# A recurrent attention and a mixture of experts in one kernel: tokens laid out eight to a partition, one stream of transposes, one state per head, and a running maximum

## The chip, the core and the metric

One NeuronCore of a Trainium2 chip. The metric is the device time of one execution in microseconds (us), lower is better. TensorE (PE) multiplies, PEld is its weight load, VectorE is DVE, ScalarE is ACT, GpSimd is POOL; SP issues DMAs. Each engine runs its own instructions in order.

## The reference

```python
r, k, v: (4, 8, 768, 48) float32     # batch, heads, tokens, head dim; w, u: (8, 48), w in 0.85 to 0.95
for t in range(S):
    cur = einsum('bhd,bhe->bhde', u[None] * kt, vt)
    y[:, :, t] = einsum('bhd,bhde->bhe', rt, state + cur)
    state = w[None, :, :, None] * state + einsum('bhd,bhe->bhde', kt, vt)
x = y.transpose(0, 2, 1, 3).reshape(3072, 384)
logits = x @ phi                                   # phi (384, 32): 8 experts x 4 slots
d = exp(logits - logits.max(0)); d /= d.sum(0)     # over the tokens, for each slot
slot_input = (d.T @ x).reshape(8, 4, 384)
slot_out[e] = maximum(slot_input[e] @ w1[e], 0) @ w2[e]   # w1 (384, 1024), w2 (1024, 384)
c = exp(logits - logits.max(1)); c /= c.sum(1)     # over the slots, for each token
out = c @ slot_out                                 # (3072, 384)
```

A softmax does not change when the same number is taken from all its logits, so a kernel may take away any maximum, or none where the logits are small. The first part is a linear recurrence: with k scaled by a falling power of w and r by the opposite one, a chunk of 128 tokens is a masked 128x128 product (A, then A times v) plus r times the state of the chunks before it.

## The kernel before

Work goes by head pairs: m counts 4 batches x 4 pairs, 16 in all; each pair's 768 tokens are split in two halves of 384 (L = 3 chunks of 128), i counting 32 half-units. The 768 tokens of a head lie six to a partition (J = 6); v lies three to a partition in each half.

- **Tables** (`table`, L175, L177): W[0] and W[1] hold the powers of w, from logarithms by Exp. `scale` (L212) multiplies k and r by them and casts to bf16, on GpSimd but for the first pair.
- **Transposes**: `t_pe` (L219) turns k and r into kT and rT, `t_evac` (L225, ScalarE) puts the tokens in order while copying; `b_pe` (L231) and `b_evac` (L236, VectorE) turn kT back into kn, now in order. `prod_f` (L241) multiplies k and r elementwise for the diagonal term.
- **v** is cast by ScalarE (`v_cast`, L250) and put in order on TensorE by products with shifted permutation matrices Q3 (`v_pe`, L265, nine per half), copied out by L271.
- **Recurrence**: `a_pe` (L280) and the mask (`mask_f`, L285); `m_pe` (L306) sums k times v into states Mb of 128x96, two heads side by side, of which `z_evac` (L320, L324) masks the two diagonal blocks with bmask; the state of the first half is carried into the second one by Z0, decayed by wT. `dv` (L326) is v times the diagonal term. `y_pe` (L336, L347, L349) sums y in Yb, `y_evac` (L356) copies it into x.
- **Routing** (`route`), eight half-units later: transposes of x (L371, L380), logits with phi (L364), Exp without a maximum (L386), its transpose into LexpT (L393, L397), and the dispatch (L404) with the sum acc (L412), once per half batch.
- **After the loop**: the last two half batches of routing, the normalised slot inputs uns (L517, L519), the experts (L535 and w1, L541 and L543, transposes L552, L553, then L557 and w2), row sums (L545), and the output: 24 products (L581) alternately scaled by VectorE (L583) and ScalarE (L585), and seven DMAs.

The order on each engine is the program's order, written out by hand: a loop over i interleaves the stages of half-units i, i+1 and i+2. All loads of k, r and v come from SP's queue, batch by batch into three buffers; the weights (cast to bf16 by the DMA) from GpSimd's queue, counted out by W_AT behind given half-units, w2 into buffers that k, r and v no longer need. PSUM is eight banks: T0, T1, Ab (two), Mb, Yb, Xb, Vb. A tile of two banks is one tile to the dependences between engines.

Of the kernel before, what the change touches and what calls it, by code (L numbers as in the profile page):

```python
# [9 lines left out]
def kernel(  # L10
# [24 lines left out]
    G = 2  # L35
    L = nC // G
    T = L * C
    P2 = 2 * D
    nN = Nn // C
    nG = B * G  # L40
    nU = B * nQ
    nH = nU * G
    J = S // C
    JV = T // C

# [4 lines left out]
    ALU = mybir.AluOpType  # L50

# [7 lines left out]
    wk = ctx.enter_context(tc.tile_pool(name="wk", bufs=3))  # L59
    psb = ctx.enter_context(tc.tile_pool(name="psb", bufs=1, space=bass.MemoryType.PSUM))  # L60


    RW = H * J * D
    NR = 3
    EG = E // 2
    raw = [big.tile([128, 3 * RW], f32, name=f"raw{j}") for j in range(NR)]
    eW2 = nF * Dm
    w1_all = big.tile([128, E, nM, F], bf, name="w1_all")

    def w2_of(e):  # L70
        g, j = divmod(e, EG)
        return raw[1 + g][:].bitcast(bf)[:, j * eW2:(j + 1) * eW2].rearrange("p (y d) -> p y d", y=nF)

    def raw_of(which, b):
        return raw[b % NR][:, which * RW:(which + 1) * RW]

    T0 = psb.tile([128, 1024], bf, name="T0")
    T1 = psb.tile([128, 1024], bf, name="T1")
    Ab = psb.tile([128, 2, 512], f32, name="Ab")
    Mb = psb.tile([128, 512], f32, name="Mb")  # L80
    Yb = psb.tile([128, 512], f32, name="Yb")
    Xb = psb.tile([128, 512], f32, name="Xb")
    Vb = psb.tile([128, 512], f32, name="Vb")
    Xh = Xb[:].bitcast(bf)
    xT_p = Xh[:, 0:Dm]
    lg_p = Xb[:, 192:192 + L * ES].rearrange("p (c s) -> p c s", c=L)
    le_p = Xh[:, 640:640 + T]
    ds_p = Mb[:, 384:384 + (nM + 1) * ES]


    LexpT = cst.tile([128, Nn], bf, name="LexpT")
    early = LexpT[:, 0:2 * (2 * H * D + 128)].bitcast(f32)
    w_row = early[0:1, 0:H * D]
    lnw = early[:, H * D:2 * H * D]
    one_f = early[0:1, 2 * H * D:2 * H * D + 128]
    warm = LexpT[:, 2048:2560]
    wu = cst.tile([8, 128], f32, name="wu")
    wu3 = wu[:].rearrange("q (e s) -> q e s", s=64)
    phi_f = cst.tile([128, nM, ES], f32, name="phi_f")
    O(act.preload_act_table_set("natural_log_exp_and_others"))  # L100
    O(sp.dma_start(out=w_row, in_=w.rearrange("(o h) d -> o (h d)", o=1)))
    O(dve.memset(one_f, 1.0))
    O(dve.memset(warm, 0.0))
    O(dve.memset(wu[:], 1.0))
    O(act.dma_start(out=wu3[0:4, :, 0:D], in_=w.rearrange("(q e) d -> q e d", e=2)))
    O(act.dma_start(out=wu3[4:8, :, 0:D], in_=u.rearrange("(q e) d -> q e d", e=2)))

    def load_kr(which, src, b, h0, h1):
        O(sp.dma_start(out=raw_of(which, b).rearrange("p (h x) -> p h x", h=H)[:, h0:h1, :],
                       in_=src[b, h0:h1].rearrange("h (p j) d -> p h (j d)", j=J)))  # L110

    def load_v(b, h0, h1):
        O(sp.dma_start(out=raw_of(2, b).rearrange("p (h x) -> p h x", h=H * G)[:, h0 * G:h1 * G, :],
                       in_=v[b, h0:h1].rearrange("h (g p j) d -> p (h g) (j d)", g=G, j=JV)))

    def load_batch(b, step):
        for h0 in range(0, H, step):
            load_kr(0, k, b, h0, h0 + step)
            load_kr(1, r, b, h0, h0 + step)
            load_v(b, h0, h0 + step)  # L120

    load_batch(0, 2)
    load_batch(1, 2)
    O(sp.dma_start(out=phi_f[:], in_=moe_phi.rearrange("(mo p) s -> p mo s", p=128)))
    load_batch(2, H)

    def load_w(n, y0=0, y1=nF):
        if n < E:
            O(pool.dma_start(out=w1_all[:, n, :, :],
                             in_=moe_w1[n].rearrange("(p mo) f -> p mo f", p=128)))  # L130
        else:
            O(pool.dma_start(out=w2_of(n - E)[:, y0:y1, :],
                             in_=moe_w2[n - E].rearrange("(p y) d -> p y d", p=128)[:, y0:y1, :]))

    def keep_warm(n, cols=512):
        for _ in range(n):
            O(pe.matmul(Yb[:, 0:cols], warm[:, 0:128], warm[:, 0:cols], start=True, stop=True))


    s_i = cst.tile([128, J], i32, name="s_i")  # L140
    O(pool.iota(s_i, pattern=[[-1, J]], base=T - 1, channel_multiplier=-J))
    ident_f = cst.tile([128, 128], f32, name="ident_f")
    O(pool.memset(ident_f[:], 0.0))
    O(pool.affine_select(out=ident_f[:], in_=ident_f[:], compare_op=ALU.not_equal, fill=1.0, base=0,
                         pattern=[[-1, 128]], channel_multiplier=1))
    QW = 2 * C + JV - 1 + C
    Q3 = cst.tile([128, QW], bf, name="Q3")
    O(pool.memset(Q3[:], 0.0))
    O(pool.affine_select(out=Q3[:], in_=Q3[:], compare_op=ALU.not_equal, fill=1.0, base=JV - 1,
                         pattern=[[-1, QW]], channel_multiplier=JV))  # L150
    mask_ut = cst.tile([128, 128], f32, name="mask_ut")
    O(pool.memset(mask_ut[:], 0.0))
    O(pool.affine_select(out=mask_ut[:], in_=mask_ut[:], compare_op=ALU.is_ge, fill=1.0, base=0,
                         pattern=[[-1, 128]], channel_multiplier=1))

    sk = cst.tile([128, J], f32, name="sk")
    O(dve.tensor_copy(sk[:], s_i[:]))
    O(dve.tensor_scalar(out=sk[64:128, :], in0=sk[64:128, :], scalar1=float(T), scalar2=None, op0=ALU.add))
    sr = cst.tile([128, J], f32, name="sr")
    O(dve.tensor_scalar(out=sr[:], in0=sk[:], scalar1=-1.0, scalar2=-1.0, op0=ALU.mult, op1=ALU.add))  # L160
    NKR = 3
    kr_t = [cst.tile([128, 2, J, 128], bf, name=f"kr{j}") for j in range(NKR)]
    for t in kr_t:
        O(dve.memset(t[:].rearrange("p a j (e s) -> p (a j e) s", s=64)[:, :, D:64], 0.0))
# [3 lines left out]
    keep_warm(5)  # L168
    O(pe.matmul(Xb[:, 0:H * D], one_f, w_row, start=True, stop=True))
    O(act.activation(out=lnw, in_=Xb[:, 0:H * D], func=AF.Ln))  # L170
    W = [cst.tile([128, nQ, J, P2], f32, name=f"W{j}") for j in range(2)]

    def table(j, q):
        e = (sk, sr)[j]
        O(dve.tensor_mul(W[j][:, q], lnw[:, None, q * P2:(q + 1) * P2].to_broadcast([128, J, P2]),  # L175
                         e[:, :, None].to_broadcast([128, J, P2])))
        O(act.activation(out=W[j][:, q], in_=W[j][:, q], func=AF.Exp))  # L177

    table(0, 0)
    table(1, 0)  # L180
    bmask = cst.tile([128, P2], f32, name="bmask")
    ones = cst.tile([128, 128], bf, name="ones")
    ucol = cst.tile([128, nQ, 2], bf, name="ucol")
    Le_t = [cst.tile([128, L, 128], bf, name=f"Le{j}") for j in range(2)]
    uns = cst.tile([128, nM, 2, EG, 32], bf, name="uns")
    O(pool.memset(bmask[:], 0.0))
    O(pool.memset(bmask[0:64, 0:D], 1.0))
    O(pool.memset(bmask[64:128, D:P2], 1.0))
    O(pool.memset(ones[:], 1.0))
    O(pool.memset(ucol[:], 0.0))  # L190
    for t in Le_t:
        O(pool.memset(t[:], 0.0))
    O(pool.memset(uns[:], 0.0))
    O(pe.transpose(Mb[:, 0:8], wu[:], ident_f[0:8, 0:8]))
# [423 lines left out]
```

## Time and profile before

| | |
|---|---|
| timed runs | 148.05, 148.68, 150.45 us, median 148.68 us |
| profiled execution | span 146.5 us from the first to the last instruction; the page states no other time for it |
| TensorE / weight loads | 105.9 us (72%) / 81.6 us, 1719 products |
| VectorE | 101.9 us (70%), 200 instructions |
| ScalarE | 83.8 us (57%), 176 |
| GpSimd | 56.5 us (39%), 68 |
| DMA | 31.77 MB moved, HBM read 39.38 MB, written 4.72 MB |
| mean granted TensorE clock | 0.947 |

Busy time is a share of the whole span and so an average over stages: a preparation to 15 us, the loop to 111 us, the last routing to 117 us, the experts to 130 us, the output to the end. Products are pipelined on TensorE, and the duration of one says little of what a further one costs; the distance between starts does. A wait is put down to the instruction that came last.

### The profile page before, as it was taken

To read this page: it belongs to the slowest core of one execution; us is meant where nothing else is said; L and a number is where in the kernel's file an instruction comes from. 1 tells how busy PE (TensorE), PEld (TensorE's weight loads), DVE (VectorE), ACT (ScalarE), POOL (GpSimd) and SP (SyncE) were. 2 spreads that over 40 slices of the span, in tenths; PEclk is the share of its full clock that TensorE was granted. 3 is DMA by queue.
4 is the path that set the end of the run, shared out by engine and by line. 5 is a ranking of instruction groups with operands and counts; after the bars stand their busy time and mean duration, and the time that the engine had idled before them with its cause. 6 is when DMAs were issued, how large, how long until landed. Compare 5 with 4: busy or idle time off the path is not lost. (4 is left out here: it accounts for less than half of the span.)

```text
span 146.5 us, 4187 instructions
## 1 busy us (share of the span) xinstructions
PE 105.9 (72%) x1719; PEld 81.6 (56%) x1719; DVE 101.9 (70%) x200; ACT 83.8 (57%) x176; POOL 56.5 (39%) x68
## 2 busy tenths in 40 slices
PE   6495795748478995987788689689596579956500
PEld 1144664546367784875777577569475437534300
DVE  5355779869999999599589689689883414228710
ACT  3327565757547886687588498398475411027610
POOL 7433333359995874576449279000000000000000
PEclk9999559999999999999999999999999959999975
DMA  4999999999940199999999999999999500006994
GB/s 96 337 372 375 370 364 376 382 327 386 368 145 2 20 190 215 214 183 214 175 174 158 184 200 172 216 215 214 215 216 206 104 0 4 0 0 269 415 416 190
DMA packets 20764, 31.77 MB, mean 217 GB/s; under 512 B 1289, under 2 KB 17674, under 8 KB 20746
## 3 DMA queue, kind: packets, MB, share of 16 engines
q0 software_dynamic: 2448, 12.58, 44.1%
q1 hardware_dynamic: 18274, 18.93, 37.4%
q8 instruction: 13, 0.21, 0.6%
q14 instruction: 5, 0.04, 0.1%
q10 hardware_dynamic: 24, 0.00, 0.0%
HBM read 39.38 MB, written 4.72 MB: 301 GB/s over the span
## 5 line engine op out<-in xcount | busy, mean ns | idle before, releaser
L212 POOL TENSOR_TENSOR kr<-raw,W 128x576 bf16<-128x576 f32 x30 | 41.9, 1412 | 31.1 <-PE T L219 15.2
L285 DVE TENSOR_TENSOR AT<-Ab,mask_ut 128x768 bf16<-128x768 f32 x32 | 30.4, 951 | 3.3 <-PE Ab L280 3.3
L265 PE MATMUL Vb<-v_bf,Q 128*128 128x96 bf16 x288 | 18.1, 210 | 7.3 <-ACT v_bf L250 7.3
L265 PEld LDWEIGHTS <-Q 128*128 128x128 bf16 x288 | 16.2, 100 | 11.5 <-issue 11.0
L225 ACT COPY kT<-T 128x768 bf16<-128x768 bf16 x16 | 12.7, 796 | 14.3 <-PE T L219 14.0
L219 PE MATMUL T<-ident,kr 128*128 128x128 bf16 x192 | 16.8, 228 | 4.3 <-POOL kr L212 4.3
L356 ACT CAST x<-Yb 128x288 bf16<-128x288 f32 x32 | 13.1, 409 | 4.6 <-PE Yb L349 4.6
L219 PEld LDWEIGHTS <-kr 128*128 128x128 bf16 x192 | 12.5, 103 | 5.1 <-POOL kr L212 4.6
L271 ACT CAST vn<-Vb 128x288 bf16<-128x288 f32 x32 | 13.1, 410 | 3.7 <-PE Vb L265 2.1
L241 DVE TENSOR_TENSOR prod<-T,kT 128x768 bf16<-128x768 bf16 x16 | 15.2, 948 | 0.1
L225 ACT COPY rT<-T 128x768 bf16<-128x768 bf16 x16 | 12.7, 797 | 3.4 <-PE T L219 2.9
L326 DVE TENSOR_TENSOR dv<-vn,Mb 128x288 bf16<-128x288 bf16 x32 | 14.2, 444 | 0.0
L236 DVE COPY kn<-T 128x768 bf16<-128x768 bf16 x16 | 8.9, 554 | 7.2 <-PE T L231 4.1
L280 PE MATMUL Ab<-rT,kT 64*128 64x128 bf16 x192 | 11.1, 222 | 2.2 <-DVE AT L285 2.1
L324 DVE TENSOR_TENSOR Z<-Mb,bmask 128x192 bf16<-128x192 f32 x32 | 11.1, 348 | 0.7 <-PE Mb L310 0.7
L306 PE MATMUL Mb<-vn,kn 128*128 128x96 bf16 (+2 forms) x80 | 11.6, 245 | 0.0
L250 ACT CAST v_bf<-raw 128x576 bf16<-128x576 f32 x16 | 10.8, 675 | 0.0
L336 PE MATMUL Yb<-vn,AT 128*128 128x48 bf16 x192 | 10.4, 186 | 0.1
L349 PE MATMUL Yb<-dv,ident 128*128 128x288 bf16 x32 | 9.2, 289 | 0.6
L347 PE MATMUL Yb<-Z,rT 128*128 128x96 bf16 x80 | 8.9, 205 | 0.5 <-DVE Z L324 0.5
L336 PEld LDWEIGHTS <-AT 128*128 128x128 bf16 x192 | 7.0, 97 | 3.6 <-DVE AT L285 0.2
L380 ACT COPY xT<-Xb 128x384 bf16<-128x384 bf16 x18 | 8.8, 486 | 0.3 <-PE Xb L371 0.2
(120 smaller groups left out, 198.9 us busy)
## 6 DMA issues: line engine op xcount, KB each, us to landing
w_all<-in_moe_w_dram POOLq DMA_DIRECT2D x8, 768.0 KB, 8.4
raw<-in_moe_w_dram POOLq DMA_DIRECT2D x7, 768.0 KB, 14.5
raw<-in_k_dram SPq DMA_DIRECT2D x8, 288.0 KB, 5.1
raw<-in_r_dram SPq DMA_DIRECT2D x8, 288.0 KB, 5.5
raw<-in_v_dram SPq DMA_DIRECT2D x8, 288.0 KB, 5.6
raw<-in_k_dram SPq DMA_DIRECT2D x2, 1152.0 KB, 8.9
raw<-in_r_dram SPq DMA_DIRECT2D x2, 1152.0 KB, 10.7
raw<-in_v_dram SPq DMA_DIRECT2D x2, 1152.0 KB, 9.9
```

Of the source, the lines that this page charges most:

```text
L212: O(eng.tensor_mul(kr[:, j].rearrange("p j (h s) -> p j h s", s=64)[:, :, :, 0:D], src, W[j][:, q].rearrange("p j (h d) -> p j h d", h=2)))
L219: O(pe.transpose(bank[:, x * C:(x + 1) * C], kr[:, j, x, :], ident[:]))
L225: O(act.copy(t[:].rearrange("p (s j) -> p s j", j=J), bank[:, 0:S].rearrange("p (j s) -> p s j", j=J)))
L241: O(dve.tensor_mul(pr[:].rearrange("p (s j) -> p s j", j=J), T1[:, 0:S].rearrange("p (j s) -> p s j", j=J), st["kT", m][:].rearrange("p (s ...
L265: O(pe.matmul(Vb[:, c * P2:(c + 1) * P2], Q3[:, o:o + C], vb[:, :, g, j, :], start=(j == 0), stop=(j == JV - 1)))
L271: O(act.copy(vn[:].rearrange("p c e d -> p (c e d)"), Vb[:, 0:L * P2]))
L280: O(pe.matmul(Ab[:, e, c * C:(c + 1) * C], kT[s, t], rT[s, t]))
L285: O(dve.tensor_mul(AT[:], Ab[:, :, 0:T].rearrange("p e (c t) -> p e c t", c=L), mask_ut[:, None, None, :].to_broadcast([128, 2, L, C])))
L306: O(pe.matmul(o, kn[:, g * L + c, :], vc, start=first, stop=True, skip_group_check=True))
L326: O(dve.tensor_mul(dv[:], st["v", i][:].rearrange("p c e d -> p (c e) d"), Mb[:, 288:288 + 2 * L, None].to_broadcast([128, L * 2, D])))
L336: O(pe.matmul(Yb[:, o:o + D], AT[:, e, c, :], vn[:, c, e, :], start=first, stop=False, skip_group_check=True))
L356: O(act.copy(st["x", n][:, :, q * P2:(q + 1) * P2], Yb[:, 0:L * P2].rearrange("p (c e) -> p c e", c=L)))
```

## The change

The first part is rewritten; the experts and the output keep their form.

- Each batch is three **tiles** x of eight tokens per partition for two heads at once (heads q and q+4 side by side: e is 0 or 1). A tile holds eight chunks of 128 tokens; a head pair's six chunks run over the tiles' borders. Seven tiles fit in the buffer; 12 tiles x 3 DMAs of 384 KB.
- A **stream of 60 steps**, five per tile: k, r and v are transposed (24 products), k and v transposed back (16). A step is eight transposes into one of two banks T and a copy out of it. The copies move two bf16 as one 4-byte element. `more` drains the stream at four places of a unit; GpSimd scales k and r, and now also casts v, one tile ahead.
- A **unit** is a head pair with all 768 tokens; the powers of w are centred on token 384, so no decay between halves is needed (Z0, wT and bmask go).
- **Compact states**: each head has its own 64x48 block on its own 64 partitions, five sums of chunks per pair (KV, RZ), made by 64-column products and used by 64-row ones; one ScalarE copy instead of masks on VectorE.
- **Running maximum**: per batch the largest logit (VectorE reduction, transpose, reduction, broadcast by a product), taken away in the Exp; the sum acc of the batches before is rescaled by fac. Routing runs once per batch.
- LexpT is laid out so that later weight loads read neighbouring elements; experts, transposes and output use separate PSUM tiles in place of the two banks of Ab.
- Matmuls in the program: 1915, against 1719; VectorE rows 142 against 198, ScalarE 131 against 181.

```diff
-    G = 2; L = nC // G; T = L * C; J = S // C      # six tokens per partition, two halves
+    J = 8; R = C // J; nX = nQ * nC // J; L = nC // 2
...
+    def step(n):
+        t, kind = divmod(n, 5)
+        bank = n % 2
+        Tb = T[bank]
+        if kind < 3:
+            kr = kr_t[kind][t % NK]
+            for j in range(J):
+                O(pe.transpose(Tb[:, j * C:(j + 1) * C], kr[:, j].rearrange("p e s -> p (e s)"), ident[:]))
+            o = wk.tile([128, J * C], bf, name=("kT", "rT", "vT")[kind], bufs=(3, 3, 1)[kind])
+            st[kind, t] = o
+            O(act.copy(o[:].bitcast(f32).rearrange("p (g j c) -> p g j c", g=J, j=J),
+                       Tf[bank].rearrange("p (j g c) -> p g j c", g=J, j=J)))
+            if kind == 1:
+                ...                                 # pr: VectorE, r (PSUM) times kT, 128x1024
+            return
+        src = st[0 if kind == 3 else 2, t]
+        for g in range(J):
+            O(pe.transpose(Tb[:, g * C:(g + 1) * C], src[:, g * C:(g + 1) * C], ident[:]))
+        ...                                         # kind 3: kn by VectorE; kind 4: vn by ScalarE
+    KV = {0: (0, 3), 1: (0, 2), 2: (0, 1), 3: (3, 2), 4: (3, 1)}
+    RZ = {1: (2,), 2: (1,), 3: (0,), 4: (0, 4), 5: (0, 3)}
+    def m_pe(i):
+        for c, (s0, n) in KV.items():
+            for e in range(2):
+                s = slice(64 * e, 64 * e + 64)
+                o, vc = Mb[s, s0 * D:(s0 + n) * D], vn[:, kap, e, 0:D]
+                ...
+                O(pe.matmul(o, kn[:, sl.start + 64 * e:sl.start + 64 * e + 64], vc, ...))
+        ...                                         # diagonal term: six 2-column products
+    def z_evac(i):
+        O(act.copy(Z[:], Mb[:, 0:nZ * D]))
+        O(dve.tensor_mul(dv[:], ...))               # 128x576
+    def y_pe(i):
+        ...                                         # 12 products AT x v into Yb[:, e]
+        for c in range(1, nC):
+            for z in RZ[c]:
+                for e in range(2):
+                    O(pe.matmul(Yb[:, e, c * D:(c + 1) * D], st[1, t][s, sl], Z[s, z * D:(z + 1) * D], ...))
+        ...                                         # two products with dv
+    def max_a(b):
+        O(dve.tensor_reduce(out=mx[:], in_=lg_p, axis=AX.X, op=ALU.max))
+        O(pe.transpose(Xb[0:1, 0:128], mx[:], ident_f[:]))
+    def max_b(b):
+        O(dve.tensor_reduce(out=g_row[:, 0:1], in_=Xb[0:1, 0:128], axis=AX.X, op=ALU.max))
+        if b:
+            O(dve.tensor_max(g_row[:, 0:1], g_row[:, 0:1], g_row[:, 1:2]))
+        O(pe.matmul(Xb[:, 128:129], one_f[:], g_row[:, 0:1], start=True, stop=True))
+    # max_c: nG = -maximum; le_ev: Exp with bias nG, fac; disp_ev: acc = acc * fac + D_p
+    W_AT = {5: 2, 6: 1, 7: 1, 8: 2, 9: 1, 10: 1, 11: 2}      # weight DMAs behind the scaling of tile t
+    def target(i, part):
+        if i < 0:
+            return 4 * (i + LEAD) + part + 1        # LEAD = 3: twelve steps ahead of unit 0
+        return 4 * LEAD + (15 * (4 * i + part + 1)) // 16
+    for i in range(-LEAD, nU):
+        b, q = divmod(i, nQ)
+        a_pe(i + 1, 0); mask_f(i + 1, 0)
+        more(target(i, 0))
+        y_pe(i); y_evac(i)
+        more(target(i, 1))
+        if b >= 1 and q == 0: lg_pe(b - 1)
+        m_pe(i + 1); z_evac(i + 1)
+        a_pe(i + 1, 1); mask_f(i + 1, 1)
+        if b >= 1 and q == 0: max_a(b - 1)
+        more(target(i, 2))
+        if b >= 1 and q == 0: max_b(b - 1)
+        if b >= 1 and q == 1: le_t(b - 1); let_ev(b - 1); disp(b - 1); disp_ev(b - 1)
+        if i >= 0 and q >= 1: xt_pe(b, q - 1); xt_ev(b, q - 1)   # 12 transposes of 64 columns
+        more(target(i, 3))
+        if b >= 1 and q == 0: max_c(b - 1); le_ev(b - 1)
...
-    hb = [[Ab[:, 0, :], Ab[:, 1, :]], [Vb[:], Yb[:]]]
+    hb = [[Yb[:, 0, :], Tf[1]], [Mb[:], Tf[0]]]
...
-    ob = [T1[:].bitcast(f32), Ab[:, 0, :], Ab[:, 1, :], T0[:].bitcast(f32), Yb[:], Xb[:]]
+    ob = [Tf[0], Tf[1], Yb[:, 0, :], Xb[:], Ab[:, 0, :], Mb[:]]
```

## The prediction

> **What bounds the kernel now.** I read the page first (its slices and its groups), then busy time by stage, then the timeline of one stretch of the main loop and of the end.
>
> ```profile
> PE   6495795748478995987788689689596579956500
> DVE  5355779869999999599589689689883414228710
> PEclk9999559999999999999999999999999959999975
> DMA  4999999999940199999999999999999500006994
> ```
>
> Forty slices of 3.66 us. The DMA engines are full to slice 11 (k, r, v), rest, are full again to 112 us (weights), and once more at the end (output). VectorE is the fullest engine from slice 9 to slice 29. The granted TensorE clock is halved in slices 5 and 6.
>
> ```profile
> core 0: us, PE busy (x) PEld busy (x) DVE busy (x) ACT busy (x) POOL busy (x), PEclk, DMA share, GB/s
> 15.00:44.00 29.00, 19.96 (x325) 16.46 (x322) 25.21 (x44) 17.52 (x33) 18.80 (x14) 0.88 1.02 338
> 44.00:111.00 67.00, 55.52 (x1092) 46.68 (x1089) 56.25 (x111) 48.85 (x109) 30.90 (x33) 1.00 0.91 177
> 117.00:130.00 13.00, 11.53 (x152) 7.06 (x148) 3.33 (x6) 1.19 (x2) 0.00 (x0) 0.87 0.01 1
> ```
>
> The loop stage (15 to 111 us) is what the change rewrites. VectorE is 84 to 87% busy there. The waits list has 15.2 us of POOL L212 behind PE L219: GpSimd is mostly ahead. The starts of L285 give the pace: the ninth stands at 43.56 us, the last at 108.72, so 24 half-units cost some 2.8 us each, 5.6 us per head pair.
>
> ```profile
> L285 DVE TENSOR_TENSOR AT<-Ab,mask_ut 128x768 bf16<-128x768 f32 x32 | 30.4, 951 | 3.3 <-PE Ab L280 3.3
> L326 DVE TENSOR_TENSOR dv<-vn,Mb 128x288 bf16<-128x288 bf16 x32 | 14.2, 444 | 0.0
> ```
>
> ```profile
> 62.15 0.34 PE L280 MATMUL Ab<-rT,kT 64*128 64x128 bf16 x6
> 62.42 0.32 PE L336 MATMUL Yb<-vn,AT 128*128 128x48 bf16 x6
> 62.59 0.24 PE L347 MATMUL Yb<-Z,rT 128*128 128x96 bf16 x2
> 70.11 0.41 PE L404 MATMUL Mb<-Le,x 128*128 128x32 bf16 x9 [1.17 <-DVE dv L326]
> 124.85 4.77 PE L557 MATMUL Mb<-raw,W 128*32 128x384 bf16 x64 [0.34 <-DVE W L553]
> ```
>
> The two VectorE rows give a line: 288 elements 444 ns, 768 elements 951 ns, so 140 ns and 1.056 ns per element. The starts of the TensorE groups give prices that durations hide: six L280 in 0.27 us (45 ns each, two 64-row halves into two banks), six L336 in 0.17 us (28 ns). In the same way a 128x128 transpose costs 57 ns, a 32-column L404 29 ns, a 2-column L310 25 ns, a 288-column L349 120 ns. L404 shows a stall: TensorE runs in order, and at a boundary of the routing it waits for VectorE.
>
> **The head.** VectorE prepares two tables of 768 instead of 576 elements (0.95 for 0.75 us) and a few small operations, so the first scaling starts at about 8.8 instead of 7.57 us. Two scalings (0.95 each), six small ones (L196: 0.17 us), a table (0.95) and its exponential (ScalarE's line through L356, 288 elements 409 ns, and L225, 768 elements 797 ns, gives 0.8) put GpSimd's first scaling at 13.6. Before unit 0 has its turn TensorE must transpose k and r of tile 2, so GpSimd first does four scalings of 768 elements (L212: 1.41 us for 576, so 1.85), one cast of v and the fills of Le and uns (L193: 0.75 us for 768, so 1.7 with ones). The cast is not in the trace: at least a fill (0.75), at most a scaling (1.88); I take 1.3, a single input. 13.6+7.4+1.3+1.7 = 24.0, with the transposes **24.5 us**. After that GpSimd owes 5.0 us per tile and 0.6 us per weight issue (L129), 0.94 tiles per unit: not the pace.
>
> **A unit of the new loop** (one head pair, all 768 tokens; 16 of them). Removed: 18 permuting matmuls and 12 + 6 transposes, the Z masks (L324 2 x 0.35, L320 0.32), v_bf and half of the small copies. Added: 3.75 steps of eight transposes, 0.46 us each; Y has 12 AT products (0.34), 14 state products of 64 rows by 48 columns, two of 288 columns (0.24); M has ten 64-column products and six of 2 columns (0.15); X has 12 half-width transposes (three units of four). These 36 partial-array instructions are not in the trace in this form. From below: windows of 1 us show 30 of L557 (32-column weights, neighbours in different column groups) between 125 and 126 us, 33 ns for 384 columns. From above: L557's mean, 4.77/64 = 75 ns. I take 25 to 30 ns, since neighbours alternate halves and stream at most 144 columns: Y 0.93, M 0.45, X 0.36.
>
> TensorE's sequence in an ordinary unit: A 0.27, step 0.46, Y 0.93, step 0.46, M 0.45, A 0.27, step 0.46, X 0.36, step 0.46 = 4.12 us. VectorE's work is 2 x 0.95 (masks), 0.75 (dv, 576 elements), and per tile 1.22 (pr, 1024) and 0.69 (kn; L553: 0.69 for the same bytes): 4.1 us per unit against 5.3 before. The tighter ring runs through both: M ends at 2.57, dv 0.75, the second mask 0.95, two hand-overs of 0.1, then Ab is free for the next unit: **4.5 us**. The unit that follows pr holds a bank 0.8 us longer: 4.6.
>
> **The running maximum and routing** come once per batch. In its first unit TensorE does 18 L360 (0.54), M ends at 3.2, then its transposition of the maximum waits for dv 0.75, mask 0.95 and the reduction (192 elements, 0.35): until 5.4; 0.3 for itself, a step 0.46, a wait for kn 0.69, two reductions 0.4 and hand-overs, 0.25 for the broadcast, a step: **8.1 us**. Queued behind these waits are all later products, and VectorE and ScalarE wait for those. In the second unit le_t 0.34, a wait of 0.95 for two ScalarE copies (0.59 and 0.49; Xb is one tile), dispatch 24 x 0.03 = 0.72, a wait of 0.4 for acc, X and the rest: **6.5 us**. A batch is 8.1+6.5+4.5+4.6 = 23.7.
>
> First batch, without routing and with phi_s (L477 cost 3.0 us as three; one pass, I take 1): 19.1. Last: 8.1, and 9.6 for three units that have no steps left: 17.7. The loop: 19.1 + 2 x 23.7 + 17.7 = 84.2, from 24.5 to **108.7**, against 111.07 now (the last L356): **-2.4**.
>
> **After the loop.** From the last copy to uns: now 5.8 us; then X, its copy, logits, the maximum's seven hand-overs, exponential, one dispatch, acc, csr, uns, 6.9: +1.1. Experts: the wait of PE Ab L535 for ACT (0.7 us) goes, since the four banks are separate tiles; the 24 row sums now read contiguous weights (L545's loads 172 ns, contiguous ones 97): -1.3 together. Output: the wait of 2.1 us of PE Ab L581 goes, but the DMA share is 1.0 from 135 us on, so only the 1 us of thin DMA at 133 can be won: -0.7. These edits lie on the chain that ends last. Loads and weights I cost at nothing: the weights take 60 us at the rate of slices 14 to 30, are fed from tile 5 on (some 38 us) and end near 105 us, w2 being needed from 115. If that cover goes, every us of lateness past 115 is a us of time.
>
> **Sum.** -2.4+1.1-1.3-0.7 = -3.3. Span 146.5 becomes 143.2. The page gives the profiled execution no time but its span; the median of the runs, 148.68, stands 2.2 above that, and I keep the 2.2: **145.4 us**. Own range of this case: 142 to 149 (a hand-over more or less, 0.1 us at six places per unit ring and boundary, and the bounds of the cast and of phi_s).
>
> [...] The 64-row group L280 is followed by the full-array L336 at 62.42, exactly six spacings after 62.15: this trace shows no price for changing the array's shape. [...] By the row a change costs nothing. [...] I go by the row.
>
> **Rivals.**
> - *The partial-array products are dear (slower).* They lie in Y and M, ahead of the ring's turn, so 24 x 16 of them count in full. At 57 ns (the rate of a full transpose) in place of 30 the loop is 384 x 0.027 = 10.4 us longer: **156**. It decides from 46 ns on (6.2 us over 384 is slower by 2%). For it: L280 costs 45 ns, L557 75 in the mean. Against: 33 ns in L557's alternating half.
> - *The boundaries cost no more than now (faster by more).* Now a batch has two stalls of 1.17+0.58 us, 3.5 in all; I give it 5.3, and the tail 1.1 more. If the maximum hides behind steps and masks as the old waits did, 1.8 x 3 + 1.1 go: **139**. For it: TensorE has four steps to fill with. Against: it is in order, and each step sits behind a wait.
> - *GpSimd sets the pace (no change).* If the cast costs as a scaling (1.88) and VectorE's two-input work slows it (one L175 took 1.18 instead of 0.75 us beside a running L212), a tile is 5.6 to 6 us, and the head and first batch lose 3 us: **148.5**. Against: ten L212 in a row took 13.69 us, undisturbed.
>
> **How the numbers follow.** Forecast 0.44 (0.23 of it below 145.7, 0.21 within 2%), dear products 0.24, cheap boundaries 0.22, GpSimd 0.10 (0.04 within, 0.06 above with other delays). 2% is 3 us, about what a measurement of this kernel can tell from no change. Faster 0.23+0.22 = 0.45, same 0.25, slower 0.30. The range reaches to 137 (cheap boundaries, somewhat better) and 156 (products at 57 ns).
>
> **What would show it.** Right: first y of unit 0 near 25 us, mask starts 4.5 us per pair in ordinary units, the transposed maximum waiting about 2 us for VectorE three times, last copy near 109, VectorE some 84 us busy instead of 102. Wrong: spacings over 46 ns in the 64-row or 64-column groups, POOL without idle time through the loop, weights landing after 115 us, or a halved clock in the boundary units.

## The result, and the profile after

The changed kernel takes **161.56 us** (median of 4 runs, 159.89 to 162.24) beside 149.56 us for the kernel before (148.05 to 150.7): ratio **1.091**, 95% interval 1.080 to 1.102. It is slower; the forecast was 145.4 us with a range of 137 to 156, so both sign and range missed. The profiled execution has a span of 160.2 us. Executions of one kernel differ by some per cent here, mostly with the granted clock (before beside e13: 148.5 us at a mean of 0.941, 156.69 us at 0.87), so ratios are taken over the shorter ones, and of the profiled executions below those of e2, e5, e8, e9, e10 and e13 were among the longer ones.

The slices of the page, 4.0 us each, the same rows as shown of before:

```profile
PE   6934779978999388889739798965978659989400
DVE  2785836568566535466552548464264032508700
PEclk9999999999999759999965999995685555999955
DMA  4999999999999750798582099999997000004994
```

VectorE is no longer the fullest engine. What is new is in the third row: the TensorE clock is cut to half three times inside the loop (slices 14 and 15, 21 and 22, 28 and 29) and through the last routing and the first products of the experts (31 to 34). Busy time by stage (from:to, length, then TensorE, its weight loads, VectorE, ScalarE and GpSimd, granted clock, DMA share, GB/s):

```profile
15.00:44.00 29.00, 23.88 (x388) 20.02 (x385) 18.30 (x23) 15.03 (x29) 26.50 (x23) 1.00 1.06 352
44.00:125.00 81.00, 64.87 (x1257) 52.62 (x1253) 43.74 (x70) 34.13 (x72) 31.50 (x32) 0.83 0.76 150
132.00:144.00 12.00, 10.71 (x152) 6.01 (x153) 3.67 (x9) 1.61 (x3) 0.00 (x0) 0.85 0.01 3
```

In the main loop TensorE has a mean clock of 0.83 where before had 1.00, and VectorE is busy 54% instead of 84%: neither is full. The groups that answer to L285 and L326 (count, busy, mean ns, idle before and its releaser):

```profile
L276 DVE TENSOR_TENSOR AT<-Ab,mask_ut 128x768 bf16<-128x768 f32 x32 | 30.4, 950 | 4.6 <-PE Ab L271 4.6
L307 DVE TENSOR_TENSOR dv<-vn,Mb 128x576 bf16<-128x576 bf16 x16 | 12.0, 752 | 19.9 <-ACT Z L304 19.9
L245 DVE TENSOR_TENSOR pr<-T,kT 128x1024 bf16<-128x1024 bf16 x12 | 8.3, 689 | 13.9 <-ACT rT L240 13.9
```

The second row holds a wait that the forecast did not have: VectorE stands 19.9 us before dv, and what ends last there is the copy of Z, which dv does not use. Only a part of that wait is the copy's: in the timeline below Z starts at 79.11 us, when the products into Mb are done, and dv at 79.50, so Z costs dv 0.39 us, some 6 us over 16 units. The rest is the wait for the products that both read.

The timeline of one batch boundary (the first unit of the third batch; idle time and its releaser in brackets):

```profile
76.53 0.47 PE L316 MATMUL Yb<-vn,AT 128*128 128x48 bf16 x12
76.93 0.34 PE L323 MATMUL Yb<-Z,rT 64*128 64x48 bf16 x14
77.21 0.42 PE L326 MATMUL Yb<-dv,ident 128*128 128x288 bf16 x2
...
78.45 0.39 PE L293 MATMUL Mb<-vn,kn 128*64 128x144 bf16 x10
78.77 0.30 PE L297 MATMUL Mb<-ucol,pr 128*128 128x2 bf16 x6
...
79.11 0.36 ACT L304 CAST Z<-Mb 128x240 bf16<-128x240 f32 x1 [0.32 <-PE Mb L297]
79.50 0.75 DVE L307 TENSOR_TENSOR dv<-vn,Mb 128x576 bf16<-128x576 bf16 x1 [1.33 <-ACT Z L304]
80.17 0.95 DVE L276 TENSOR_TENSOR AT<-Ab,mask_ut 128x768 bf16<-128x768 f32 x1
81.04 0.35 DVE L364 TENSOR_REDUCE mx<-Mb 128x1 f32<-128x192 f32 x1
81.44 0.37 PE L365 MATMUL Xb<-ident_f,mx 128*1 128x128 f32 x1 [2.10 <-DVE mx L364]
81.61 1.06 PE L251 MATMUL T<-ident,kT 128*128 128x128 bf16 x8
...
83.82 0.58 PE L371 MATMUL Xb<-g_row,one_f 1*128 1x1 f32 x2 [1.15 <-DVE g_row L370]
84.33 1.03 PE L251 MATMUL T<-ident,vT 128*128 128x128 bf16 x8
```

It shows three things. Fourteen L323 take 0.28 us from start to start (20 ns each) and ten L293 0.32 us (32 ns): the partial-array products are about as cheap as forecast (25 to 30 ns). The twelve half-width transposes L343 take 0.46 us (38 ns) in an ordinary unit, where 0.36 was forecast. TensorE stands 2.10 us for the reduction and 1.15 us for the maximum, as forecast. And then eight transposes take 1.06 us where they take 0.61 in ordinary units: half clock, which lasts here until 87.96 (granted clock 0.51 from 84 to 88 us).

The first product of each pair (L271) gives the sum. The head ends at 28.20 us (forecast 24.5: +3.7); the batches take 20.9, 27.1 and 27.4 us (19.1, 23.7, 23.7: +1.8, +3.4, +3.7) and the last one 22.0 (17.7: +4.3). The last y copy ends at 125.58 instead of 108.7, 16.9 us late. After it the forecast held: 6.96 us to uns (6.9), experts -1.6 us (-1.3), output -0.3 (-0.7). The first of these is partly luck, since it was priced at full clock and came out at half clock (0.50 from 126 to 132 us); in the run e12 below, with more of its clock there, the same path takes 6.5 us.

### The profile page after: what moved, and what is told of

Its sections match the earlier page's. It is cut to its first block, busy times and chain, and to the rows that moved or that the text cites. A ratio compares the mean times of both kernels' runs of the same rounds, so it can differ in the third digit from the quotient of the medians.

```text
span 160.2 us, 4435 instructions
## 1 busy us (share of the span) xinstructions
PE 118.8 (74%) x1922; PEld 90.0 (56%) x1922; DVE 83.0 (52%) x141; ACT 64.2 (40%) x126; POOL 63.9 (40%) x70
## 4 chain that ended last, share of the span: by engine, by line
PE 47%; DVE 25%; ACT 12%; issue 9%; DVEq 0%; ACTq 0%
PE T L251 7%; DVE AT L276 7%; PE T L237 5%; PE Yb L326 4%; PE Yb L316 4%; DVE w_all L575 4%; PE Yb L323 3%; PE Ab L271 3%; DVE W L172 3%; PE Mb L549 3%; ACT Z L304 3%; DVE pr L245 2%; DVE kn L255 2%; ACT x L333 2%; PE Mb L293 2%
## 5 line engine op out<-in xcount | busy, mean ns | idle before, releaser
L198 POOL TENSOR_TENSOR kr<-raw,W 128x768 bf16<-128x768 f32 x22 | 39.6, 1819 | 27.3 <-PE T L237 21.3
L237 PE MATMUL T<-ident,kr 128*128 128x128 bf16 x288 | 25.8, 245 | 3.6 <-ACT kT L240 1.4
L237 PEld LDWEIGHTS <-kr 128*128 128x128 bf16 x288 | 21.2, 112 | 7.0 <-issue 4.5
L307 DVE TENSOR_TENSOR dv<-vn,Mb 128x576 bf16<-128x576 bf16 x16 | 12.0, 752 | 19.9 <-ACT Z L304 19.9
L333 ACT CAST x<-Yb 128x576 bf16<-128x576 f32 x16 | 10.2, 639 | 17.2 <-PE Yb L326 17.2
L245 DVE TENSOR_TENSOR pr<-T,kT 128x1024 bf16<-128x1024 bf16 x12 | 8.3, 689 | 13.9 <-ACT rT L240 13.9
L271 PE MATMUL Ab<-rT,kT 64*128 64x128 bf16 x192 | 12.2, 238 | 3.3 <-DVE AT L276 3.3
L196 POOL CAST kr<-raw 128x768 bf16<-128x768 f32 x12 | 10.5, 874 | 4.1 <-DMA raw<-in_v_dram 4.1
L255 DVE COPY kn<-T 128x512 f32<-128x512 f32 x12 | 8.2, 686 | 6.5 <-PE T L251 6.5
L251 PE MATMUL T<-ident,kT 128*128 128x128 bf16 x96 | 9.5, 257 | 1.8 <-DVE pr L245 1.7
L271 PEld LDWEIGHTS <-kT 64*128 64x128 bf16 x192 | 6.6, 100 | 5.6 <-issue 4.2
L251 PE MATMUL T<-ident,vT 128*128 128x128 bf16 x96 | 9.5, 258 | 0.0
L316 PE MATMUL Yb<-vn,AT 128*128 128x48 bf16 x192 | 8.8, 196 | 0.6 <-DVE AT L276 0.6
L343 PE MATMUL Xb<-ident,x 128*64 128x128 bf16 x144 | 7.0, 238 | 2.2 <-DVE acc L407 1.0
L316 PEld LDWEIGHTS <-AT 128*128 128x128 bf16 x192 | 7.4, 105 | 1.8 <-issue 0.8
## 6 DMA issues: line engine op xcount, KB each, us to landing
raw<-in_moe_w_dram POOLq DMA_DIRECT2D x7, 768.0 KB, 16.9
```

Source lines behind the costliest of these rows:

```text
L196: O(eng.tensor_copy(kr, src))
L198: O(eng.tensor_mul(kr, src, W[w_][:, x]))
L237: O(pe.transpose(Tb[:, j * C:(j + 1) * C], kr[:, j].rearrange("p e s -> p (e s)"), ident[:]))
L245: O(dve.tensor_mul(pr[:].rearrange("p (g j c) -> p g j c", g=J, j=J), Tb[:].rearrange("p (j g c) -> p g j c", g=J, j=J), st[0, t][:].rearr ...
L251: O(pe.transpose(Tb[:, g * C:(g + 1) * C], src[:, g * C:(g + 1) * C], ident[:]))
L255: O(dve.tensor_copy(o[:].bitcast(f32), Tf[bank]))
```

## The experiments

The first theory put the excess down to the running maximum at the boundaries; the rivals were the head and the ordinary units. Runs are called by the short names that the expectations use. Each ratio is to the kernel before, run beside it; its median there was 149.6 to 152.4 us.

**Without the maximum (e1).**

```
-  Exp(lg_p, bias=nG)   max_a, max_b, max_c   acc = acc*fac + D
+  Exp(lg_p)                                  acc = acc + D
```

> The running maximum is left out: Exp has no bias, acc is only added up; nothing else changes. Theory A (the maximum's waits, and the halved clock that follows them, make most of the loss): each first unit of a batch falls from 9.0 to about 5.8 us (no transpose, no reduction, no broadcast), the second from 8.0 to about 7 because its first products run at the full clock, the tail after the loop loses 2.5 us and the half clock: 3 x 4.2 + 4 = 16 to 17 us, time 144 to 147. Theory B (the ordinary unit, 5.0 to 5.3 us where 4.5 was forecast, makes it): only the bare operations go, 3 x 2 us, time 154 to 156.

Measured 142.43 us (142.16 to 146.32), ratio to before 0.953 (0.941 to 0.965). The boundary's first unit falls from 8.9 to 4.9 us, and the loop has no halved clock (eight transposes take 0.61 to 0.62 us all through it). The maximum, with the halved clock behind it, costs this kernel 19 us: more than the 12 us that it loses to the kernel before.

**The waits kept, TensorE kept busy in them (e3):** dummy products stand in the two pauses of three boundaries.

```
 max_a:  reduce(mx)
+        34 x matmul(Yb, ident, ident)
         transpose(mx) ...
+        20 x matmul(Yb, ident, ident)
         matmul(Xb, one_f, g_row)
```

> The waits for the maximum stay, but TensorE gets useless 128-column products to do in them (34 ahead of the transposition, 20 ahead of the broadcast, into the free Yb), in the three boundaries inside the loop. Theory A (the clock halves because TensorE idles there, and that costs by itself): granted clock 1.0 through all three boundaries, first units 9.0 to about 8.2, second 8.0 to about 7.0, time 155 to 157. Theory B (the half clock is hidden under the waits): 161 to 162, or 163 if the filling is longer than the waits.

155.03 us (153.39 to 155.69), ratio 1.037 (1.022 to 1.052). The transposition of the maximum comes as late as before (2.44 us behind the start of L271, 2.43 before), but the first boundary's units take 7.8 and 7.0 us instead of 8.9 and 8.0, and the clock row has its first halved slice at 111 us (six L271 take 0.44 us from start to start at 111.69, 0.27 before that). So the halved clock alone was some 6 us: the time fell by 6.5, of which 0.6 lies ahead of any fill (the first unit took 4.5 instead of 5.1 us). At full clock the forecast's 8.1 for the first unit was about right.

**The maximum early (e4):** all of it kept, the reduction right behind the logits, its small products ahead of the second mask, the broadcast behind the last step.

```
 lg_pe(b-1)
+reduce(mx)
 m_pe, z_evac, a_pe(i+1, 1)
+transpose(mx); reduce(g_row); max with the last
 mask_f(i+1, 1)
 ... steps ...
+matmul(Xb, one_f, g_row)      # was between the steps
```

> The maximum is kept, its operations are moved in program order: the reduction right behind the logits and ahead of dv and the mask, the small reductions ahead of the second mask, the broadcast behind the last step of the unit. Theory A (TensorE stands in order behind VectorE's queue): TensorE waits under 0.5 us in place of 2.1 and 1.2, clock stays at 1.0, first units 9.0 to 6.3, second 8.0 to 7.0, time 150 to 153. Theory B (the number of operations and hand-overs costs, not their place): 159 to 162.

149.41 us (147.15 to 151.58), ratio 0.987 (0.974 to 0.999). TensorE's waits for VectorE's small operations all but go, first units take 5.6 to 5.8 us. Twelve us by the medians (14 by e4's two shortest executions, 147.15 and 147.45) were thus the place of some ten instructions in an in-order queue, the halved clock behind them included.

**dv ahead of Z (e2)**, against the 19.9 us of waiting.

```
-  act.copy(Z, Mb)
   dve.tensor_mul(dv, vn, ds_p)
+  act.copy(Z, Mb)
```

> One exchange in program order: VectorE's dv is recorded before ScalarE's copy Z of the states. Both read the PSUM tile Mb, and in the trace dv starts only after Z (19.9 us of waits in all). Theory A (the ring M, Z, dv, mask, A sets the ordinary unit): 0.45 us less in some 12 units, time 155 to 157. Theory B (the ring has slack behind TensorE's own work): within 1 us of 161.6. Theory C (Z is now late for Y): slower.

161.98 us (158.89 to 163.31): no gain is shown; the shortest execution is 1.0 us below the shortest of the changed kernel. In the profiled one (162.28 us) the pairs of the first batch come ever earlier (the fifth at 47.10 instead of 49.13 us), and then the clock is halved in five stretches of the loop instead of three (eight transposes in up to 1.06 us there, 0.61 to 0.62 elsewhere); it alone can't say whether that always happens. The edit was tried again on e4, where the maximum's pauses are gone (e6):

> e4 (the maximum's operations recorded earlier; 149.4 us) and in it the copy of the running states Z recorded behind the product dv, so that VectorE reads the bank Mb first. Theory T (two engines that read one bank of PSUM take turns, and dv waited .4 to .5 us for Z in every unit, which stands in the ring product, dv, mask, product): the wait of dv for Z, 17.4 us in 13 rows of e4, goes; eleven ordinary units shorten from 5.0 to about 4.6 us, and the time falls to 144 to 146. Rival U (Z is needed as early as dv, by the products of the states into Yb, so the wait only changes its name): the wait moves to ACT Z behind DVE dv and to PE behind Z, units stay at 5.0, time 148 to 151.

150.07 us (148.55 to 151.28), ratio 1.022 (1.011 to 1.033), where e4 alone had 149.41 (0.987). Units are again short (4.1, 5.6, 4.6, 5.0 against 4.5, 5.6, 5.0, 5.3 us), and neither theory had what takes it back. The second units of the second and third batch take 8.3 and 9.1 us instead of 7.3 and 7.4. In the third batch:

```profile
80.45 0.36 ACT L308 CAST Z<-Mb 128x240 bf16<-128x240 f32 x1 [1.47 <-DVE dv L306]
81.73 0.66 PE L403 MATMUL Xb<-Le,x 128*128 128x32 bf16 x18 [1.75 <-ACT LexpT L396]
83.86 1.03 PE L251 MATMUL T<-ident,kT 128*128 128x128 bf16 x8
```

The same stands in a run with the maximum left out, dv first and a filled head (e9), whose expectation was:

> The maximum left out as in the first experiment (142.4 us), with dv ahead of Z and the fill products in the head. If the terms add: 142.4 - 4 - 3 = 135 to 137. Rival (the transfer of the experts' second weights, which ended the chain of the first experiment at 113.5 us, decides: it can only come earlier by what the last cast of v, at 80.8 us there, comes earlier): the experts start at the last cast + 32.7 us; with the cast 3 us earlier by the head alone, 139 to 140.

It took 144.83 us (142.97 to 146.71), ratio 0.966 (0.949 to 0.982): no better than e1 without these two edits (142.43, ratio 0.953). Its timeline at the second unit of a batch:

```profile
57.31 0.36 ACT L308 CAST Z<-Mb 128x240 bf16<-128x240 f32 x1 [1.47 <-DVE dv L306]
...
57.57 0.59 ACT L240 COPY vT<-T 128x512 f32<-128x512 f32 x1
...
58.05 0.50 ACT L390 COPY LexpT<-Xb 128x384 f32<-128x384 f32 x1
...
58.59 0.64 PE L397 MATMUL Xb<-Le,x 128*128 128x32 bf16 x18 [1.75 <-ACT LexpT L390]
...
60.63 1.03 PE L251 MATMUL T<-ident,kT 128*128 128x128 bf16 x8
```

ScalarE now stands 1.47 us in front of Z; behind Z in its queue are vT and LexpT; TensorE waits 1.75 us for LexpT (0.78 with Z first), and the clock is halved for over 6 us (0.50 from 59 to 65 us). The wait was not removed but moved to a queue with something urgent behind it.

**The head (e5).** Eight of its transposes take 1.01 us although the clock row reads full. The kernel before had the same sign, there in the clock row too (0.53 from 14.65 to 21.97 us):

```profile
17.21 0.82 PE L219 MATMUL T<-ident,kr 128*128 128x128 bf16 x6 [0.75 <-POOL kr L212]
17.82 0.85 PE L231 MATMUL T<-ident,kT 128*128 128x128 bf16 x6
```

Six transposes take 0.61 us there from start to start, 102 ns each. The run e5:

```
 step(s)
+if s < 10: 14 x matmul(Yb, ident, ident)
```

> The changed kernel as it is, with fourteen 128-column products into a bank that nothing reads yet added behind each of the first ten transposing steps. Theory H (the head was late because TensorE's clock was still low while it waited for GpSimd: the 24 transposes of the steps took 100 to 109 ns each until about 30 us, although the profile's row of granted clock says full): the first attention product of the unit loop starts near 25 us instead of 28.2, transposes take about 57 ns from the third step on, and the time falls by 2.5 to 3.7 us, to 158 to 159. Rival H2 (the head is late by GpSimd's or VectorE's work, or the eight-token layout's transposes simply cost 100 ns there): the first product stays at 28 us or comes later by the fill, time 161 to 163.

The timeline of TensorE in the changed kernel:

```profile
20.97 1.87 PE L237 MATMUL T<-ident,kr 128*128 128x128 bf16 x16 [1.20 <-ACT vn L258]
22.77 0.50 PE L271 MATMUL Ab<-rT,kT 64*128 64x128 bf16 x6
23.39 1.01 PE L251 MATMUL T<-ident,kT 128*128 128x128 bf16 x8
```

The same stretch with the fill (L435):

```profile
21.00 0.61 PE L237 MATMUL T<-ident,kr 128*128 128x128 bf16 x8 [0.82 <-ACT vn L258]
21.44 0.94 PE L435 MATMUL Yb<-ident 128*128 128x128 bf16 x14
22.22 0.61 PE L237 MATMUL T<-ident,kr 128*128 128x128 bf16 x8
```

Half of the theory stands: with the fill, transposes run at full rate (eight in 0.61 us). But from 21 us on TensorE had next to no idle time until 28 us, and each 0.78 us of fill stood in its way: the loop starts at 29.11 us instead of 28.20. The time of 163.22 us (159.53 to 163.9) shows no gain. The same fill together with the early maximum and dv first (e7):

> The three edits together: the maximum's operations early, dv ahead of Z, and the fill products in the head; the maximum is kept. If the terms add (12 us for the first, about 4 for the second, about 3 for the third): 161.6 - 19 = 142 to 144. Rival (the experts' second half of weights is bound by its transfer: it is issued behind the last cast of v and landed 32 us after it where the maximum was left out, 81.6 to 113.5 us, so the end follows that cast and not the units): the chain ends with the transfer into raw, time 145 to 147.

150.78 us (149.49 to 152.26), ratio 1.012 (0.997 to 1.027), no better than e4: the fill in the way, and halved stretches behind pauses of 1.75 us as in e9. On e4 with the fill behind the first five steps only (e10):

> e4 (the maximum's operations early; its profiled execution had the first product of the unit loop at 27.74 us) and the fourteen fill products behind the first five transposing steps only, where TensorE waits for GpSimd and ScalarE anyway. The run with the fill behind ten steps showed the first half of theory H (transposes at 57 ns with the fill, 100 to 131 without) and not the second: from the sixth step on TensorE had no idle left, and each fill of .78 us stood in its way. Theory H': without those five fills (3.9 us) the first product comes at 25 to 25.5 us, the fill itself costs nothing, and the time falls by 2 to 2.7 us to about 147. Rival: GpSimd's pace takes the gain back within the first batch (a later product waits for kr), time 149 to 150.

The loop starts at 26.37 instead of 27.74 us: 1.4 us from transposes at full rate, some half of what was expected. The time of 149.63 us (146.77 to 149.94) does not show it, and the shortest execution is only 0.4 us below e4's. The profiled one (149.94) had a halved stretch from 82.91 us, behind waits of 0.78 and 0.52 us (eight transposes in 1.03 us); waits of 0.78 and 0.51 us left the clock alone in e4's (0.62 us).

**LexpT early (e11, on e4):** its transposes and copy ahead of m_pe and Z in the unit.

```
 more(target(i, 1))
+if b >= 1 and q == 1: le_t(b-1); let_ev(b-1)
 m_pe(i+1); z_evac(i+1)
 ...
-le_t(b-1); let_ev(b-1)
 disp(b-1)
```

> e4 with the six transposes of the exponentials and their copy (LexpT) recorded one part earlier, ahead of the unit's products into Mb and the copy of Z. Theory S (the second unit of a batch takes 7.3 us because the dispatch products wait .8 us for LexpT, queued on ScalarE behind Z and the copy of vT, and not because of its own 42 products): the wait of PE for LexpT goes, the second units of the three batches shorten from 7.3 to 6.4 to 6.6 us, time 146.5 to 148. Rival: the wait moves to Z and dv (ScalarE has the same copies to make), second units stay at 7.2 to 7.4, time 149 to 150.

147.3 us (146.92 to 148.32), ratio 0.986 (0.980 to 0.992), against 0.987 for e4: the times show no gain. Second units do take 6.9 us instead of 7.3 (6.4 to 6.6 were expected): the wait for LexpT is gone, but one of 0.9 us for acc stands behind it.

**Maximum early, LexpT early, dv first, fill behind five steps (e12):**

> Maximum kept and early, LexpT early, dv ahead of Z, and fill behind the first five steps. In e6 and e7 dv ahead of Z shortened the ordinary units to 4.6 to 5.0 us, but ScalarE then waited 1.5 us for dv with LexpT behind it, TensorE stood 1.75 us, and in four of the six profiled cases of the three batches the clock was halved for 4 to 6 us after it. Theory G (a gap of 1.7 us or more in TensorE's work at a batch boundary halves the clock): with LexpT ahead of Z no gap of over 1.2 us is left in the loop, no transpose takes over 80 ns after 26 us, and the time is 149.4 - 2.4 (head) - 2.5 (second units) - 3 to 4 (dv) = 141 to 142, unless the second weights bind (last cast of v + 32.7 us): then 143. Rival: the clock is halved by something else (heat, or the share of busy time), then stretches of half clock stay: 147 to 150.

**141.27 us** (140.11 to 143.39), ratio 0.942 (0.931 to 0.953): a version that computes everything and beats both kernels, 20 us below the changed one. Its clock row, slices of 3.5 us, is full from slice 6 to slice 31:

```profile
PEclk9996899999999999999999999999999559999855
```

**The same with Z first again (e15):**

> e12 with one edit taken back: the copy of Z is recorded ahead of dv again, as in the changed kernel. Theory T (ScalarE and VectorE take turns on the bank Mb, and dv waits .4 to .5 us for Z in each unit): ordinary units 5.0 us again instead of 4.6, dv waits for Z 15 us or more in sum, time 144.5 to 146.5. Rival U (the order of the two doesn't matter, and e12's time is that of the early LexpT and the fill): 141 to 142.

147.66 us (146.22 to 147.88). From its waits list (total, times, longest):

```profile
DVE dv L307 <- ACT Z L304: 17.8, 13, 1.9
```

And from that of e12:

```profile
ACT Z L308 <- DVE dv L306: 15.7, 16, 1.6
```

The pair takes turns either way (each sum also holds the wait for the products that both read). With dv first the fourteenth pair starts at 94.63 us, with Z first at 98.64: 4.0 us of loop for the order of two instructions. The rest lies behind that, where e15's clock is 0.50 from 106 us to the experts at 117.2 (0.79 in e12 from 101.5 to 111.2); that the order causes this too is not shown.

**e12 without the maximum (e13):**

> e12 (141.3 us) with the running maximum left out, as in the first experiment. It prices the maximum where its operations stand early and no gap is left. Theory: what is left of it is the reduction and three small operations on VectorE, of which little lies on the ring: 139 to 141, or bound by the second weights (last cast of v + 32.7 us). Rival: the chain reduce, transpose, reduce, broadcast still holds the first unit of each batch by 1 us or more (5.2 us against 4.9 without it), and le_ev behind it: 136 to 138.

136.73 us (135.59 to 139.59): the rival's time holds. The maximum still costs some 4.5 us when placed well. Of this the three first units show 0.6 to 0.9 us each (4.5 to 4.8 instead of 5.2 to 5.4), less than the rival's 1 us; where the rest lies is not shown.

**What halves the clock (e14):** three pauses in e12, away from boundaries.

```
+if i in {3: 3, 7: 1, 11: 2}:   # so many reductions of 768 numbers
+    gs = reduce(W[0]);  matmul(Yb, gs, ident)
 y_pe(i)
```

> e12 with three pauses of TensorE of different length put in on purpose, in ordinary units of the first, second and third batch: VectorE reduces a table of 768 numbers three times, once and twice (an estimated .9 us each, from .35 us for 192), and a product that reads the result stands ahead of the unit's output products; the work of the kernel is otherwise the same. Theory G (a pause of about 1.7 us or more halves the clock for 4 to 6 us, a pause of up to 1 us doesn't): after the triple one (2.7 us) and after the double one (1.8 us) the transposes take 100 to 131 ns for 4 to 7 us, after the single one 57; the time is that of e12 plus the pauses (5.4 us) plus 2.5 to 3 us for each halved stretch: 151 to 153. Rival (the clock is halved by something of the batch boundary, such as the fp32 transposes or the many short products, and not by the pause): no half clock behind any of the three, time 146 to 147.

The timeline, each pause (in brackets at L464) and products behind it:

```profile
45.47 0.24 PE L464 MATMUL Yb<-ident,gs 128*64 128x128 bf16 x1 [3.85 <-DVE gs L463]
...
46.93 1.06 PE L251 MATMUL T<-ident,vT 128*128 128x128 bf16 x8
...
48.69 0.50 PE L271 MATMUL Ab<-rT,kT 64*128 64x128 bf16 x6
49.12 0.71 PE L237 MATMUL T<-ident,kr 128*128 128x128 bf16 x8
...
70.49 0.24 PE L464 MATMUL Yb<-ident,gs 128*64 128x128 bf16 x1 [1.72 <-DVE gs L463]
...
71.60 0.61 PE L251 MATMUL T<-ident,vT 128*128 128x128 bf16 x8
...
95.49 0.24 PE L464 MATMUL Yb<-ident,gs 128*64 128x128 bf16 x1 [2.70 <-DVE gs L463]
...
96.60 0.61 PE L251 MATMUL T<-ident,vT 128*128 128x128 bf16 x8
...
98.34 1.03 PE L237 MATMUL T<-ident,kr 128*128 128x128 bf16 x8
```

152.28 us (one execution). VectorE's queue made the pauses longer than planned. Those of 3.85 and 2.70 us are followed by half clock for about 3 us each (granted clock 0.50 from 46 to 48 and from 98 to 100 us), the second only some 1.7 us after the work has resumed; that of 1.72 us, which the theory would have had halve it, is not (1.00 from 70 to 74 us). So a pause is enough by itself, with no fp32 transpose and no boundary near. But 1.75 us at a boundary, followed within 1 us of work by another 0.45 to 0.52, halved it in five of the six cases in e6, e7 and e9. The sum of waits over some microseconds fits these cases better than one gap, but not e10's, where half clock followed 0.78 and 0.52 us once; the rule stays open.

**The kernel before with separate banks in the experts and six in the output (e8).**

```
-hb = [[Ab0, Ab1], [Vb, Yb]];   ob = [T1, Ab0, Ab1, T0, Yb, Xb]
+hb = [[Ab0, T1], [Vb, Yb]];    ob = [T1, Ab0, Vb, T0, Yb, Xb]
```

> The kernel before, with the banks of the experts' first stage and of the output chosen as in the changed kernel (each of the two rectifiers has a bank of its own; no two engines read one bank in turn). Forecast term: experts -1.3 us and output -.7 us in the changed kernel, of which the experts' part was put down to the rectifiers of ScalarE and VectorE in one bank. If so: stage from the first product on w1 to the first output 12.0 to 12.5 us instead of 13.5, time lower by .7 to 1.5 us. Rival (the gain came from the layout of w1's and LexpT's operands, not the banks): same within .5 us.

148.81 us (146.22 to 153.59), ratio 0.987 (0.981 to 0.993). Its timeline of the first stage of the experts:

```profile
118.95 1.04 PE L535 MATMUL Ab<-w_all,uns 128*32 128x512 bf16 x12 [0.74 <-DMA raw<-in_moe_w_dram]
119.76 1.51 PE L535 MATMUL T<-w_all,uns 128*32 128x512 bf16 x12
```

The second group follows the first without a wait, where before had one of 0.75 us. The experts' stage takes 13.05 us instead of 13.53 (12.0 to 12.5 were expected), the output 15.3 instead of 16.1. So banks give some -0.5 of the changed kernel's -1.6 us in the experts; the rest is about what the row sums lose, from 1.84 us (24 L545 of before) to 0.75 us (24 L537) with contiguous operands, an edit that no run takes alone. Why the changed kernel's output gains 0.3 us where e8's gains 0.8 is open.

## Why the prediction was wrong, step by step

- **Boundaries (8.1 and 6.5 us).** The waits were right (2.10 us, "about 2"), the operations too. The failing step is that a price at full clock was put on units in which TensorE stands over 3 us: "a halved clock in the boundary units" stood in the list of signs and had no price. It cost some 6 us in three boundaries (e3). In the last batch, 4.3 us late, the clock is half from 108.98 to 115.44 and again from 118.53 on; the stretch behind 118.53 was not filled and so is not shown apart. At full clock the second unit still took 7.0 us, 0.5 more than forecast; ScalarE's queue ahead of LexpT is 0.4 us of this (e11).
- **The ring (4.5 us).** "M ends at 2.57, dv 0.75, the second mask 0.95, two hand-overs of 0.1" (one from VectorE to TensorE, L364 to L365 in the boundary above, took 0.05) left out the copy of Z between M and dv, about 0.4 us in every unit: the changed kernel has 5.0 and 5.3, e12 with dv first 4.6 and 5.05. By e15 this term is 4.0 us over the loop. The unit behind pr was forecast at 4.6, so 0.4 us of it stays open; pr itself was over-sized: 689 ns, not 1.22 us.
- **The head (24.5 us).** GpSimd was on time (first scaling 13.7, cast of v 0.87 us against 1.3 taken), but was not the limit. TensorE's transposes cost about twice the 57 ns that were taken (eight in 0.81 us, 101 ns each, and sixteen in 1.80, 113 ns), although the page of before, read for its halved slices 5 and 6, had them at 102 ns in its own head; filling recovers 1.4 us of the 3.7. Of the rest 1.7 us is the chain of unit 0 itself: even in e12 its last mask ends at 26.14 and the loop starts at 26.19 us. The forecast let the loop start when the last transposes were done. The remaining 0.6 us is not located.
- **The rivals.** Dear products: false (20 to 38 ns, where 46 would have decided). "The boundaries cost no more than now" (139 us) comes near e12, not this kernel; what was put against it ("each step sits behind a wait") was the decisive line. GpSimd sets the pace: false, POOL idles 27.3 us before L198, 21.3 of it for TensorE's transposes. (Its load was put at 0.94 tiles per unit; 3.75 steps of five to a tile are 0.75, so it had more slack than was said.)
- **Right:** the tail in sum (0.9 us less was forecast, 0.8 came), the experts, partial-array prices, and no price for changing the array's shape (fourteen 64-row L323 take 0.28 us up to the full-array L326 behind them, 20 ns each; the twelve full-array L316 ahead of them 0.40 us, where 0.34 was forecast). The weights did end late (last issue 98.23 us; the DMA row is full to slice 30 and partly in slice 31, up to 124 us, instead of 105), but the loop was later still; without the maximum (e1) this transfer ended the chain at 113.5 us, so the cover named in the forecast was thin.

## What to carry to other kernels

A short serial chain (reduce, transpose, reduce, broadcast) costs little in itself (some 4.5 us for four batches in e12 against e13), and much if its instructions stand in in-order queues ahead of work that does not need it (12 us of the changed kernel, e4): record each where its input is ready anyway, and look what is queued behind every waiting instruction. Price the pauses of TensorE twice, as time and as clock (the clock was some 6 us of three boundaries, e3); put at full clock only what follows steady work (behind the pauses of 3.85 and 2.70 us of e14, eight transposes took 1.06 and 1.03 us instead of 0.61). When an edit shortens a unit and the time stays, look for the queue that inherited the wait.

## What the runs showed of the hardware

- TensorE's clock was lower behind waits of 3.85 and 2.70 us alone (e14: granted clock 0.50), and mostly behind 1.75 us with 0.45 to 0.52 us soon after (five of six in e6, e7 and e9: eight transposes in 1.01 to 1.06 us); 1.72 us alone left it at 1.00 (e14, 70 to 74 us). One kernel falls on either side from batch to batch (e6: one of two pauses of 1.75 us), and one stretch in e10 followed waits of only 0.78 and 0.52 us.
- The granted-clock row read 1.00 while transposes ran at about half rate (changed kernel, 15 to 26 us: 1.01 us for eight, 0.61 with a fill in e5); durations of a known instruction were the better clock here.
- Two engines that only read one PSUM bank take turns here: in the changed kernel dv waits 0.39 us for the copy of Z, 0.36 us long, and in e12 Z waits for dv (15.7 us in sum, with the wait for the products). The wait is for a semaphore of the other engine, and no run here lets the two overlap, so whether the bank alone would have kept them apart is not shown.
